# Attention with its division moved behind the product with the values

## The chip, the cores and the metric

The kernel runs on one core of a Trainium2 chip. Five engines work side by side, each through its own list of instructions in order: PE (TensorE, matrix products and transposes into PSUM), DVE (VectorE), ACT (ScalarE), POOL (GpSimd) and SP (SyncE, which issues the transfers). They wait for each other by semaphores. The metric is the device time of one launch in microseconds; lower is better.

## The reference, cut to what matters

```python
def sm_attn(qq, kk, vv):                       # on means of 4 rows: 144 x 144 per head
    s = scale * np.matmul(qq, kk.transpose(0, 1, 3, 2))
    a = np.exp(s - np.max(s, axis=-1, keepdims=True))
    a = a / (np.sum(a, axis=-1, keepdims=True) + 1e-09)
    return np.matmul(a, vv)
out_up = np.repeat(sm_attn(q_d, k_d, v_d), 4, axis=2)
...
scores = np.where(mask, scale * q @ k.T, -1e9)  # 576 x 576 per head, |i - j| < 4
attn = np.exp(scores - max); attn = attn / (sum + 1e-09)
x = out_up + attn @ v                           # (2, 8, 576, 64) -> 1152 rows of 512
...
x = (h * tanh(softplus(h))) @ w_out             # h = x @ w_in, 2048 wide
out = sum over 8 experts of P[:, e] * (relu(x @ w1[e]) @ w2[e])
```

Batch 2, 8 heads, 576 positions, head width 64. The attention is a small part of the arithmetic; the two feed-forward stages behind it are most of it.

## The kernel before

**Stages.** A start (attention of the first 288 tokens), then a feed-forward stage whose products are mixed with the rest of the attention, then the experts. The feed-forward goes through chunks: `gemm1(s)` is 12 products (L506) into a PSUM bank of the tag `w`, `mish` the activation over ACT, POOL and DVE (L486 to L494), and `gemm2(s-4)` 12 products (L529) into banks of the tag `acc`. Large products are done in two parts (hi and lo) for accuracy.

**Units.** Attention is cut into units of three steps: `sc` (scores, row maxima, exponentials), `tr` (transposes to bring the keys onto the partitions) and `av` (product with the values). A `lunit` is 96 queries of the local attention against a window of 102 keys, 8 heads; there are 12. A `gunit` is 72 averaged queries of 4 heads against 144 averaged keys; there are 8. `softmax` (L294 to L308) takes the maxima (L300), runs one exponential for each head with its sum as a by-product (L302, the sums go to the tile `den`, named `ld` or `gd`), adds 1e-9 (L304), takes reciprocals (L305) and multiplies the exponentials by them (L307): two DVE operations a unit, one for each parity `par` of the heads, on 96 x 408 or 72 x 288 numbers. `tr` transposes by PE (L379, L335) and ACT copies the result out (L380, L337). `av` multiplies by the values (L386, L347). For a gunit ACT copies the result to `odT` (L349); for a lunit DVE adds `odT` to it (L392), ACT rounds it to `xhi` (L393) and DVE takes the rest to `xlo` (L394). `xhi` and `xlo` are what L506 reads.

**Waves.** Three waves follow the start. Wave i does three lunits and two gunits, with the transposes of q and k (`prep`, L267), while chunks 6i to 6i+5 of the feed-forward run. At the end of a wave what is left of its steps is issued before the next chunk, since that chunk reads the tokens of the wave (chunks 0, 6, 12 and 18 are the first to read new tokens). The third wave is followed by chunks without attention.

**What sets the order.** Python writes the steps into slots between the products (`pump`), and a scheduler in the framework then orders the instructions on each engine by its own model of time, so that an edit also changes the order around it. Banks of the tag `w` (4 of them) are shared by scores, transposes, `av`, `prep` and `gemm1`; a bank of `gemm1` is held until L490. In the start, short products of a constant (`warm`, L442) fill PE's gaps.

**Weights of the feed-forward** arrive as 64-bit numbers and are converted by ACT (L180) and DVE (L181, L183, L184), then split (L190, L191); the buffers that they arrive in are two, so a transfer waits for the L184 that read the buffer last.

Of the kernel before, what the change touches and what calls it, by code (L numbers as in the profile page):

```python
# [7 lines left out]
F32 = mybir.dt.float32  # L8
# [3 lines left out]
AF = mybir.ActivationFunctionType  # L12
ALU = mybir.AluOpType
# [25 lines left out]
def attn_moe_moe_kernel(  # L39
# [62 lines left out]
    POOL.affine_select(out=maskb, in_=maskb, pattern=[[-1, W + 6]], base=9, channel_multiplier=1,  # L102
                       compare_op=ALU.is_ge, fill=NEG)
    vwt = [at.tile([W, H, D], F32, name=f"vw{i}", bufs=1) for i in range(VWB)]
    pl = [at.tile([TQ, H // 2, W], F32, name=f"pl{i}", bufs=1) for i in range(PBL)]
    pg = [at.tile([SH, H // 4, SD], F32, name=f"pg{i}", bufs=1) for i in range(PBG)]
    DVE.memset(two, 2.0)
    DVE.memset(ones, 1.0)
# [185 lines left out]
    def softmax(s3, p, rows, tag):  # L294

        n, nh, nk = s3[0].shape
        den = new(at, [n, 2, nh], F32, tag + "d", 2)
        for par in range(2):
            nm = new(at, [n, nh], F32, tag + "m", 4)
            DVE.tensor_reduce(out=nm, in_=s3[par], axis=AX.X, op=ALU.max, negate=True)  # L300
            for i in range(nh):
                exps.append(ACT.activation(out=p[par][:, i], in_=s3[par][:, i], func=AF.Exp, bias=nm[:, i:i + 1],  # L302
                                           scale=1.0, accum_out=den[:, par, i:i + 1]))
        DVE.tensor_scalar(out=den, in0=den, scalar1=1e-9, scalar2=rows, op0=ALU.add, op1=ALU.mult)  # L304
        DVE.reciprocal(out=den, in_=den)  # L305
        for par in range(2):
            DVE.tensor_tensor(  # L307
                out=p[par], in0=p[par], in1=den[:, par].unsqueeze(2).to_broadcast([n, nh, nk]), op=ALU.mult)  # L308

    def gunit(b, half, q4):  # L310


        u = {}
        hps = (2 * q4, 2 * q4 + 1)

        def sc():
            bks = [at_bank() for _ in range(2)]
            for i, hp in enumerate(hps):
                for par, bk in enumerate(bks):
                    o = slice(64 * par, 64 * par + 64)  # L320
                    PE.matmul(out=bk[:SH, SD * i:SD * i + SD], lhsT=qd[b, half][o, hp, :], rhs=kd[b][o, hp, :],
                              start=True, stop=True)
            for par in range(2):
                u[par] = pg[state["pg"] % PBG]
                state["pg"] += 1
            softmax([bk[:SH, 0:2 * SD].rearrange("p (a b) -> p a b", b=SD) for bk in bks], u, 4.0, "g")

        def tr():
            u["pt"] = new(at, [W, 8 * TQ], F32, "pt", 2)[:SH, 0:8 * SH].rearrange("p (a b) -> p a b", a=8)
            for par in range(2):  # L330
                bk = at_bank()
                for i in range(2):
                    for c in range(2):
                        j = 2 * i + c
                        PE.transpose(out=bk[:SH, SH * j:SH * j + SH], in_=u[par][:, i, SH * c:SH * c + SH],  # L335
                                     identity=ident[:SH, :SH])
                ACT.activation(out=u["pt"][:, 4 * par:4 * par + 4, :].rearrange("p a b -> p (a b)"),  # L337
                               in_=bk[:SH, 0:4 * SH], func=AF.Copy)

        def av():  # L340
            if (b, half) not in odT:
                odT[b, half] = new(at, [128, HP, SH], F32, "odT", 1)
            bk = at_bank()
            for i, hp in enumerate(hps):
                for c in range(2):
                    for par in range(2):
                        PE.matmul(out=bk[64 * par:64 * par + 64, SH * i:SH * i + SH], lhsT=vd[b, c][:, 2 * hp + par, :],  # L347
                                  rhs=u["pt"][:, 4 * par + 2 * i + c, :], start=(c == 0), stop=(c == 1))
            ACT.activation(out=odT[b, half][:, hps[0]:hps[0] + 2, :].rearrange("p a b -> p (a b)"),  # L349
                           in_=bk[:, 0:2 * SH], func=AF.Copy)  # L350
        return [sc, tr, av]

    def lunit(t):
# [6 lines left out]
        def sc():  # L360
# [7 lines left out]
                    PE.matmul(out=s3[par][:, hp, :], lhsT=qT[b, half][o, hp, TQ * t3:TQ * t3 + TQ],  # L368
                              rhs=kT[b][o, hp, lo:hi], start=False, stop=(hp == HP - 1))
            for par in range(2):  # L370
                u[par] = pl[(2 * t + par) % PBL]
            softmax(s3, u, 1.0, "l")

        def tr():
            u["pt"] = new(at, [W, 8 * TQ], F32, "pt", 2)
            for par in range(2):
                bk = at_bank()
                for i in range(HP):
                    PE.transpose(out=bk[:W, TQ * i:TQ * i + TQ], in_=u[par][:, i, :], identity=ident[:TQ, :TQ])  # L379
                ACT.activation(out=u["pt"][:, 4 * TQ * par:4 * TQ * par + 4 * TQ], in_=bk[:W, 0:4 * TQ], func=AF.Copy)  # L380

        def av():
            bk = at_bank()
# [5 lines left out]
            y4 = bk[:, 0:KD * TQ].rearrange("p (a s r) -> p a s r", a=KD, r=4)  # L389
            g = odT[b, half][:, :, 24 * t3:24 * t3 + 24]  # L390
            hi_, lo_ = (z[:, :, TQ * t:TQ * t + TQ] for z in (xhi, xlo))
            DVE.tensor_tensor(out=y4, in0=y4, in1=g.unsqueeze(3).to_broadcast([128, KD, 24, 4]), op=ALU.add)  # L392
            ACT.activation(out=hi_, in_=y, func=AF.Copy)  # L393
            DVE.tensor_tensor(out=lo_, in0=y, in1=f32(hi_), op=ALU.subtract)  # L394
# [497 lines left out]
```

## Time and profile before

| | us |
|---|---|
| median of 3 runs | 1111.71 (1108.79 to 1116.67) |
| the profiled execution | 1111.02 |
| its span | 1109.2 |
| PE busy | 1077.7 (97%) |
| DVE busy | 579.6 (52%) |
| ACT busy | 487.8 (44%) |
| POOL busy | 368.9 (33%) |

The span is the time from the first to the last instruction in the profile; 1.8 us of the execution lie outside of it. PE is counted as busy also while products in flight drain and while it works at half its clock, so its share doesn't say that it is at its peak. The attention is over at about 186 us of the span, and everything behind it is alike before and after the change.

### The profile page before, as it was taken

How to read it: one execution, taken by the hardware profiler on the slowest of the kernel's cores; microseconds unless marked ns; L12 is line 12 of the kernel's file. 1: busy time of each engine (PE TensorE's matmuls, PEld its weight loads, DVE VectorE, ACT ScalarE, POOL GpSimd, SP SyncE). 2: the span in 40 equal slices, each digit the busy share in tenths (PEclk: the TensorE clock that was granted, in tenths of full speed). 3: DMA queues.
4: the chain of work that ended last, by engine and by line, in shares of the span. 5: the costliest groups of instructions: out<-in, count | busy, mean ns of one | idle time of the engine just before them, and what ended most of it. 6: DMA issues, size and time to landing. Idle time of an engine off the chain costs nothing.

```text
span 1109.2 us, 18583 instructions
## 1 busy us (share of the span) xinstructions
PE 1077.7 (97%) x7184; PEld 983.7 (89%) x7184; DVE 579.6 (52%) x1229; ACT 487.8 (44%) x1375; POOL 368.9 (33%) x406
## 2 busy tenths in 40 slices
PE   8889999999998999999999999999999999999998
PEld 7768789999998888988989898999888999889897
DVE  4877885545347554454454544435454444444442
ACT  3776777534446443424344242442424434243430
POOL 2444523402217335705134150431505224051300
PEclk9888999999999999999999999999999999999999
DMA  8374320222002102112011111201112011120002
GB/s 189 107 154 120 102 81 20 77 80 74 20 1 76 58 1 77 39 38 76 13 66 39 38 40 38 76 19 58 39 38 76 20 58 38 39 71 20 25 1 86
DMA packets 60196, 63.48 MB, mean 57 GB/s; under 512 B 24204, under 2 KB 44620, under 8 KB 60108
## 3 DMA queue, kind: packets, MB, share of 16 engines
q1 hardware_dynamic: 60108, 62.30, 18.8%
q8 instruction: 56, 0.92, 0.3%
q14 instruction: 32, 0.26, 0.1%
HBM read 59.93 MB, written 2.36 MB: 56 GB/s over the span
## 4 chain that ended last, share of the span: by engine, by line
PE 87%; DVE 4%; ACT 3%; POOL 2%; DMA 2%; issue 1%; POOLq 0%; DVEq 0%
PE w L821 36%; PE acc L783 26%; PE w L506 9%; PE acc L529 8%; PE w L783 4%; PE w L368 1%; ACT pl L302 1%; DMA raw<-in_k_dram 1%; PE acc L442 1%; DMA raw<-in_moe_w_out_dram 0%; POOL wc L695 0%; PE w L363 0%; PE w L379 0%; ACT raw L180 0%; POOL me L487 0%
## 5 line engine op out<-in xcount | busy, mean ns | idle before, releaser
L821 PE MATMUL w<-wc,hhi 128*128 128x512 f32 x1152 | 361.9, 393 | 0.0
L821 PEld LDWEIGHTS w<-wc,hhi 128*128 128x128 f32 x1152 | 210.4, 188 | 37.8
L821 PE MATMUL w<-wc,hlo 128*128 128x512 f32 x576 | 225.2, 391 | 0.0
L695 POOL TENSOR_TENSOR wc<-raw,wc 128x512 fp32r<-128x512 f32 x64 | 82.0, 1305 | 356.1 <-ACT wc L694 355.9
L783 PE MATMUL acc<-thi,wb 128*128 128x288 f32 x768 | 169.0, 295 | 0.0
L783 PE MATMUL acc<-xhi,wb 128*128 128x288 f32 x768 | 167.2, 295 | 1.7 <-DVE xlo L557 1.7
L832 DVE SCALAR_TENSOR_TENSOR yacc<-w,P,yacc 128x512 f32<-128x512 f32 x126 | 94.3, 749 | 81.1 <-PE w L821 81.1
L783 PEld LDWEIGHTS acc<-thi,wb 128*128 128x128 f32 x768 | 128.4, 188 | 3.1
L783 PEld LDWEIGHTS acc<-xhi,wb 128*128 128x128 f32 x768 | 128.1, 188 | 3.1 <-DVE xlo L557 1.9
L821 PEld LDWEIGHTS w<-wc,hlo 128*128 128x128 f32 x576 | 108.1, 188 | 23.8
L770 ACT ACTIVATE p<-acc 128x288 f32<-128x288 f32 x128 | 52.3, 410 | 143.2 <-PE acc L783 139.3
L774 ACT ACTIVATE hhi<-acc 128x288 fp32r<-128x288 f32 x128 | 52.3, 410 | 141.5 <-PE acc L783 117.3
L783 PE MATMUL acc<-xlo,wb 128*128 128x288 f32 x384 | 113.5, 295 | 0.0
L783 PE MATMUL acc<-tlo,wb 128*128 128x288 f32 x384 | 113.1, 295 | 0.0
L683 POOL TENSOR_TENSOR wb<-sums,wb 128x256 fp32r<-128x256 f32 x128 | 93.6, 748 | 53.5 <-ACT wb L682 52.1
L683 POOL TENSOR_TENSOR wb<-raw,wb 128x256 fp32r<-128x256 f32 x96 | 72.5, 758 | 97.4 <-PE acc L783 55.5
L775 DVE SCALAR_TENSOR_TENSOR hlo<-acc,hhi 128x288 fp32r<-128x288 f32 x128 | 58.2, 455 | 77.4 <-ACT hhi L774 74.9
L506 PE MATMUL w<-xhi,hi 128*128 128x288 f32 x256 | 79.4, 311 | 5.3 <-ACT xhi L393 2.9
L506 PE MATMUL w<-xlo,hi 128*128 128x288 f32 x256 | 77.7, 304 | 0.1
L529 PE MATMUL acc<-glo,hi 128*128 128x288 f32 x256 | 76.1, 303 | 1.4 <-POOL glo L494 1.4
L506 PE MATMUL w<-xhi,lo 128*128 128x288 f32 x256 | 77.3, 302 | 0.0
L796 DVE TENSOR_TENSOR acc<-acc,u 128x288 f32<-128x288 f32 x64 | 29.6, 464 | 87.7 <-PE acc L783 87.7
(192 smaller groups left out, 1992.9 us busy)
## 6 DMA issues: line engine op xcount, KB each, us to landing
raw<-in_moe_w_dram SPq DMA_DIRECT2D x64, 512.0 KB
raw<-in_moe_w_in_dram SPq DMA_DIRECT2D x16, 512.0 KB
raw<-in_moe_w_out_dram SPq DMA_DIRECT2D x16, 512.0 KB
vw<-in_v_dram SPq DMA_DIRECT2D x12, 192.0 KB
raw<-in_v_dram SPq DMA_DIRECT2D x8, 288.0 KB
raw<-in_q_dram SPq DMA_DIRECT2D x12, 144.0 KB
out_dram<-yacc SPq DMA_DIRECT2D x6, 256.0 KB
raw<-in_k_dram SPq DMA_DIRECT2D x2, 576.0 KB
```

What stands on the lines that cost most here:

```text
L302: exps.append(ACT.activation(out=p[par][:, i], in_=s3[par][:, i], func=AF.Exp, bias=nm[:, i:i + 1], scale=1.0, accum_out=den[:, par, i:i + ...
L506: PE.matmul(out=bk, lhsT=a[:, kk, o], rhs=b[:, kk, c0:c0 + n], start=(i == 0), stop=(i == 3 * KD - 1))
L529: PE.matmul(out=bk, lhsT=a[:, h, o], rhs=b, start=(first and i == 0), stop=(end and i == 2))
L683: POOL.tensor_tensor(out=t[:, 1], in0=src[u][w], in1=f32(t[:, 0]), op=ALU.subtract)
L695: POOL.tensor_tensor(out=t[:, 1], in0=r[:, a], in1=f32(t[:, 0]), op=ALU.subtract)
L770: ACT.activation(out=t, in_=bk[u, b], func=AF.Copy)
L774: ACT.activation(out=hi, in_=y, func=AF.Relu)
L775: DVE.scalar_tensor_tensor(out=lo, in0=y, scalar=0.0, in1=f32(hi), op0=ALU.max, op1=ALU.subtract)
L783: PE.matmul(out=bk[u, b], lhsT=wb[2 * h + u, w][:, wz, kk, :], rhs=ops[xz][:, k + kk, o + c:o + c + NP], start=(m < 3 and i == 0), stop=(i ...
L796: DVE.tensor_tensor(out=bk[u, "C"], in0=bk[u, "C"], in1=kept[u, "u2"], op=ALU.add)
L821: PE.matmul(out=bk, lhsT=a[:, f, 128 * j:128 * j + 128], rhs=w[:, b, :], start=(i == 0), stop=(i == 3 * FH - 1))
L832: DVE.scalar_tensor_tensor(out=y, in0=bk, scalar=p, in1=y, op0=ALU.mult, op1=ALU.add)
```

## The change

The exponentials go undivided into the transposes and the product with the values. The reciprocals of the sums are laid out over partitions by PE: in `spread`, a product with the column of reciprocals, repeated 64 times, as the weights and the identity as the moving operand puts the reciprocal of each query into 64 partitions of a PSUM bank. A lunit does 8 such products (64 x 96) in `tr`, into a bank of its own, which ACT copies into the exponentials' tile (now 128 partitions high); in `av` DVE multiplies the product with the values by it. A gunit does 4 (64 x 72) in `av`, into the free half of the same bank, and DVE multiplies `odT` by them in place, after ACT's copy. The tiles of sums have 4 buffers instead of 2.

```diff
     def softmax(s3, p, rows, tag):
...
-        den = new(at, [n, 2, nh], F32, tag + "d", 2)
+        den = new(at, [n, 2, nh], F32, tag + "d", 4)
...
         DVE.reciprocal(out=den, in_=den)
+        return den
+
+    def spread(bk, c, den, i):
+
+        n = den.shape[0]
         for par in range(2):
-            DVE.tensor_tensor(
-                out=p[par], in0=p[par], in1=den[:, par].unsqueeze(2).to_broadcast([n, nh, nk]), op=ALU.mult)
+            PE.matmul(out=bk[64 * par:64 * par + 64, c:c + n], lhsT=den[:, par, i:i + 1].to_broadcast([n, D]),
+                      rhs=ident[:n, :n], start=True, stop=True)
...
-            ACT.activation(out=odT[b, half][:, hps[0]:hps[0] + 2, :].rearrange("p a b -> p (a b)"),
-                           in_=bk[:, 0:2 * SH], func=AF.Copy)
+                spread(bk, 2 * SH + SH * i, u["den"], i)
+            z = odT[b, half][:, hps[0]:hps[0] + 2, :].rearrange("p a b -> p (a b)")
+            ACT.activation(out=z, in_=bk[:, 0:2 * SH], func=AF.Copy)
+            DVE.tensor_tensor(out=z, in0=bk[:, 2 * SH:4 * SH], in1=z, op=ALU.mult)
...
                 ACT.activation(out=u["pt"][:, 4 * TQ * par:4 * TQ * par + 4 * TQ], in_=bk[:W, 0:4 * TQ], func=AF.Copy)
+            bk = at_bank()
+            for hp in range(HP):
+                spread(bk, TQ * hp, u["den"], hp)
+            u["r"] = pl[2 * t % PBL].rearrange("p a b -> p (a b)")[:, 0:KD * TQ]
+            ACT.activation(out=u["r"], in_=bk[:, 0:KD * TQ], func=AF.Copy)
...
+            DVE.tensor_tensor(out=bk[:, 0:KD * TQ], in0=bk[:, 0:KD * TQ], in1=u["r"], op=ALU.mult)
             DVE.tensor_tensor(out=y4, in0=y4, in1=g.unsqueeze(3).to_broadcast([128, KD, 24, 4]), op=ALU.add)
```

Thirteen lines are added, so a line of the new kernel has a higher number: the spread is L312, the lunit's ACT copy L392, its multiplication L404, the gunit's L357, and old L379, L386, L392, L394, L488, L490, L506 and L529 are L386, L398, L405, L407, L501, L503, L519 and L542.

The scheduler's order changes with it. First, DVE in the first wave, where the first lunit's sums are done; `ld` are the lunit's sums, `lm` its maxima, `raw` a weight under conversion, `mm` a step of mish. Before:

```order
L304 TENSOR_SCALAR ld<-ld 96x8
L305 RECIPROCAL ld<-ld 96x8
L300 TENSOR_REDUCE lm<-w 96x4
L307 TENSOR_TENSOR pl_94<-pl_94,ld 96x408
L307 TENSOR_TENSOR pl_95<-pl_95,ld 96x408
L300 TENSOR_REDUCE lm<-w 96x4
L181 TENSOR_SCALAR raw<-raw 128x512
L488 SCALAR_TENSOR_TENSOR mm<-me 128x288
```

The same place now:

```order
L304 TENSOR_SCALAR ld<-ld 96x8
L305 RECIPROCAL ld<-ld 96x8
L300 TENSOR_REDUCE lm<-w 96x4
L181 TENSOR_SCALAR raw<-raw 128x512
L300 TENSOR_REDUCE lm<-w 96x4
L183 SCALAR_TENSOR_TENSOR raw<-raw_860,raw 128x512
L184 SCALAR_TENSOR_TENSOR raw<-raw_860,raw 128x512
L501 SCALAR_TENSOR_TENSOR mm<-me 128x288
```

The two multiplications are gone, and mish's step has come behind all three steps of the weight's conversion instead of the first.

Second, PE at the end of the second wave; `vw` are the values of a unit's window. Before, the product with the values of the last two lunits is followed by the first product of the next wave's tokens:

```order
L379 MATMUL w<-ident,pl_98 102x96 x4
L379 MATMUL w<-ident,pl_99 102x96 x4
L386 MATMUL w<-pt,vw_92 64x96 x8
L386 MATMUL w<-pt,vw_93 64x96 x8
L506 MATMUL w<-xhi,hi_797 128x288
```

Now 12 products of `gemm2` stand between, of which the first five are:

```order
L386 MATMUL w<-ident,pl_99 102x96 x4
L312 MATMUL w<-ident,ld 64x96 x8
L398 MATMUL w<-pt,vw_92 64x96 x8
L398 MATMUL w<-pt,vw_93 64x96 x8
L542 MATMUL acc<-ghi,hi_1446 128x288 x4
L542 MATMUL acc<-glo,hi_1446 128x288
```

At the end of the third wave it is the other way about: 12 products of `gemm2` stood there before, and 8 do now. Third, DVE at that end, from the second lunit's `av` on. Before:

```order
L392 TENSOR_TENSOR w<-w,odT 128x384 x2
L488 SCALAR_TENSOR_TENSOR mm<-me 128x288
L394 TENSOR_TENSOR xlo<-w,xhi 128x4x96
L490 TENSOR_TENSOR me<-mm,w 128x288
L394 TENSOR_TENSOR xlo<-w,xhi 128x4x96
```

Now:

```order
L404 TENSOR_TENSOR w<-w,pl_96 128x384
L501 SCALAR_TENSOR_TENSOR mm<-me 128x288
L405 TENSOR_TENSOR w<-w,odT 128x384
L404 TENSOR_TENSOR w<-w,pl_98 128x384
L503 TENSOR_TENSOR me<-mm,w 128x288
L405 TENSOR_TENSOR w<-w,odT 128x384
L407 TENSOR_TENSOR xlo<-w,xhi 128x4x96
L505 TENSOR_TENSOR me<-me,ml 128x288
L407 TENSOR_TENSOR xlo<-w,xhi 128x4x96
```

Between the last `av` and the last `xlo` one multiplication and mish's last step have been added.

## Rows read from the trace of the kernel before

**Rows 1.** Windows by stage: us, busy by engine (x count), PEclk, DMA share, GB/s.

```profile
37.00:47.90 10.90, 8.65 (x100) 7.23 (x100) 8.80 (x17) 8.59 (x21) 4.29 (x3) 0.71 0.46 146
47.90:98.50 50.60, 44.85 (x334) 39.30 (x334) 38.92 (x79) 33.98 (x119) 20.02 (x18) 0.79 0.52 119
98.50:146.50 48.00, 41.70 (x388) 36.33 (x386) 41.19 (x86) 35.54 (x128) 24.47 (x26) 1.00 0.46 128
146.50:186.50 40.00, 39.02 (x353) 35.25 (x353) 30.17 (x69) 29.89 (x114) 11.63 (x12) 0.96 0.15 46
186.50:1109.20 922.70, 911.26 (x5595) 836.76 (x5595) 438.24 (x931) 361.13 (x915) 295.34 (x326) 1.00 0.14 46
```

**Rows 2.** Windows by shorter stretches, where the granted clock is low; columns as above.

```profile
59.40:65.50 6.10, 6.10 (x23) 5.45 (x24) 5.06 (x11) 3.92 (x16) 2.08 (x2) 0.50 0.89 163
...
79.20:91.40 12.20, 12.20 (x83) 10.40 (x81) 9.26 (x17) 7.25 (x28) 4.57 (x4) 0.58 0.25 87
...
144.80:150.20 5.40, 3.69 (x22) 3.69 (x23) 4.92 (x11) 3.09 (x8) 0.80 (x1) 0.74 0.35 77
```

**Rows 3.** Groups of instructions by line and shape: count, busy us, mean ns of one.

```profile
L307 DVE TENSOR_TENSOR pl<-pl,ld 96x408 f32<-96x408 f32 x24 | 17.4, 762 | 0.3
...
L380 ACT ACTIVATE pt<-w 102x384 f32<-102x384 f32 x21 | 9.8, 491 | 3.9 <-PE w L379 2.9 <-PE acc L386 1.1
...
L307 DVE TENSOR_TENSOR pg<-pg,gd 72x288 f32<-72x288 f32 x16 | 8.6, 577 | 0.1
...
L392 DVE TENSOR_TENSOR w<-w,odT 128x384 f32<-128x384 f32 x10 | 5.5, 561 | 2.5 <-PE w L386 2.3
```

**Rows 4.** Timeline of PE in the first wave: start, us, what, idle before.

```profile
76.78 0.87 PE L379 MATMUL w<-ident,pl 96*102 96x96 f32 x8 [0.75 <-ACT pl L302]
78.82 0.40 PE L506 MATMUL w<-xhi,hi 128*128 128x288 f32 x1 [1.17 <-DVE me L490]
...
79.21 0.44 PE L506 MATMUL w<-xhi,lo 128*128 128x288 f32 x1
79.45 0.44 PE L506 MATMUL w<-xhi,hi 128*128 128x288 f32 x1
```

**Rows 5.** Timeline of DVE at the same place.

```profile
74.75 1.86 DVE L307 TENSOR_TENSOR pl<-pl,ld 96x408 f32<-96x408 f32 x2
...
78.33 0.44 DVE L490 TENSOR_TENSOR me<-mm,w 128x288 f32<-128x288 f32 x1
```

**Rows 6.** The chain that ended last, in order of time, third wave.

```profile
176.42 0.65 PE w L347 x16
...
178.42 0.81 PE w L386 x16
...
184.25 0.57 DVE w L392
...
186.00 0.48 DVE xlo L394
...
186.53 0.53 PE w L506 x2
```

**Rows 7.** Timeline of PE at the end of the third wave.

```profile
182.30 0.30 PE L506 MATMUL w<-xlo,hi 128*128 128x288 f32 x1
182.44 0.29 PE L506 MATMUL w<-xhi,lo 128*128 128x288 f32 x1
182.66 1.54 PE L386 MATMUL w<-pt,vw 102*64 102x96 f32 x32
```

**Rows 8.** Timeline of PE at the end of the second wave.

```profile
143.24 1.54 PE L386 MATMUL w<-pt,vw 102*64 102x96 f32 x32
146.51 0.40 PE L506 MATMUL w<-xhi,hi 128*128 128x288 f32 x1 [1.73 <-ACT xhi L393]
```

**Rows 9.** Timeline of PE in the second wave, at the first gunit's transposes.

```profile
121.80 0.41 PE L335 MATMUL w<-ident,pg 72*72 72x72 f32 x4 [0.23 <-DVE pg L307]
122.61 0.45 PE L335 MATMUL w<-ident,pg 72*72 72x72 f32 x4 [0.40 <-DVE pg L307]
```

**Rows 10.** The chain that ended last, at the end of the start.

```profile
42.41 4.26 DMA raw<-in_moe_w_out_dram
```

More of the change, by code (lines that the diff above doesn't have):

```diff
@@ L104, in attn_moe_moe_kernel @@
     vwt = [at.tile([W, H, D], F32, name=f"vw{i}", bufs=1) for i in range(VWB)]
-    pl = [at.tile([TQ, H // 2, W], F32, name=f"pl{i}", bufs=1) for i in range(PBL)]
+    pl = [at.tile([128, H // 2, W], F32, name=f"pl{i}", bufs=1) for i in range(PBL)]
     pg = [at.tile([SH, H // 4, SD], F32, name=f"pg{i}", bufs=1) for i in range(PBG)]
@@ L325, in sc @@
                 state["pg"] += 1
-            softmax([bk[:SH, 0:2 * SD].rearrange("p (a b) -> p a b", b=SD) for bk in bks], u, 4.0, "g")
+            u["den"] = softmax([bk[:SH, 0:2 * SD].rearrange("p (a b) -> p a b", b=SD) for bk in bks], u, 4.0, "g")
         def tr():
@@ L370, in sc @@
             for par in range(2):
-                u[par] = pl[(2 * t + par) % PBL]
-            softmax(s3, u, 1.0, "l")
+                u[par] = pl[(2 * t + par) % PBL][:TQ]
+            u["den"] = softmax(s3, u, 1.0, "l")
         def tr():
```

## The prediction

> **What bounds the kernel now.** I read the windows by stage first [rows 1]. Behind 186.5 us the change touches nothing, and PE fills that part: 911.26 of 922.70 us. What can move is the 186 us ahead of it. There the stages differ. In the third wave (146.5 to 186.5) PE is busy 39.02 of 40.00 us and DVE 30.17: PE sets the time. In the first wave (47.9 to 98.5) PE counts as busy for 44.85 of 50.60 us, but at a granted clock of 0.79, and in the second it is busy 41.70 of 48.00 with DVE at 41.19: in these two the waits between the engines set a good part. Then come the timelines at the places where PE waits, to see for whom. The reader is to see that L307, which the change removes, stands directly in front of PE only in three places [rows 4, 5, 9], and that the ends of the waves hang on DVE and ACT behind the product with the values [rows 6, 8]. Two stretches of the first wave run at half clock, 6.10 us at 0.50 and 12.20 us at 0.58 [rows 2]; in the second of them products start 0.24 us apart, against 0.14 at full clock [rows 4, 7], and it begins after PE has stood still twice within three us [rows 4].
>
> **What the change removes, adds and moves.**
>
> DVE loses 24 x 0.762 + 16 x 0.577 us = 17.4 + 8.6 = 26.0 us, and gains 12 multiplications of the shape of L392, 12 x 0.561 = 6.7 us [rows 3], and 8 smaller ones, which have no row: between nothing and a L392, I take half of one, 8 x 0.28 = 2.2 us. Net 17 us less, where DVE is busy for 119 us between 37 and 186.5 [rows 1]. That is worth something only where DVE is in front of PE.
>
> ACT gains 12 copies of the shape of L380, 12 x 0.491 = 5.9 us [rows 3]. Its share of the waves is 67 to 75% [rows 1], and nothing needs the copy until the multiplication in `av`, a whole step later, so I cost it at nothing in the waves. If that cover is gone, a lunit's end comes 0.49 us later.
>
> PE gains the spread. A lunit's is 8 products with 64 columns of weights and 96 moving columns of 4-byte numbers, as the 8 of its `av`: in the trace 16 records, since each such product is recorded twice, and 0.81 us from the first to what follows [rows 6]. A gunit's is 4 products of the kind of L347, half of a row of 0.65 us, 0.33 us [rows 6]. A wave has three lunits and two gunits: 3 x 0.81 + 2 x 0.33 = 3.1 us a wave, and as much in the start; 12.4 us in all. All of them hang on the reciprocals (L305), which come earlier than L307's result did, so PE should not wait for them.
>
> PE is also made to change between products over the whole array and products over half of its columns more often, at up to 12 places and twice at each. The row shows what the change costs: L386 starts 0.22 us behind the last L506, which started 0.14 us behind the one ahead of it [rows 7], so about 0.09 us. This is inside the 0.81 us, which reaches from what precedes L386 to what follows it. The Trainium skill, TensorEngine Tiling, section Key Properties, has a rule that speaks against this change: a change of the tiling mode drains TensorE. It gives no price; its result is a rival below.
>
> *Start.* PE's extra 3.1 us fall into 37 to 47.9, where the granted clock is 0.71 and PE has 2.25 us to spare [rows 1]: 3.1 / 0.71 - 2.25 = 2.1 us at worst. Against it, the last wait of this stage is a transfer of weights that takes 4.26 us [rows 10] and starts when DVE has converted the weights ahead of it, behind divisions of two lunits (4 x 0.762 = 3.0 us at most) that are no longer there; I read it as about 1 us earlier at best, since ACT's exponentials, which stay, are in front of the same conversion. Between -1.0 and +2.1 I take +0.5.
>
> *First wave.* +3.1 us for PE. Two waits should go. At 76.78 PE had waited 0.75 us for what the row calls ACT's exponentials, long done: it was L307, whose two operations run from 74.75 to 76.61 [rows 4, 5]. At 78.82 it had waited 1.17 us for a bank that L490 frees [rows 4], and L490 came late because it is queued on DVE behind the same L307 [rows 5]. In the new order L490 stands behind L184 as well, but PE has 1.1 us of spread ahead of that bank. Together -1.9 us. The clock: the 12.20 us at half speed that follow cost 6.1 us, and the stillness that preceded them is filled. Whether the clock then holds can't be read; I take it that the stretch shrinks to the length of the other one of this wave, 6.10 us, which saves 3.05 [rows 2]. Bounds: nothing, and the whole 6.1. The wave: 3.1 - 1.9 - 3.05 = -1.9.
>
> *Second wave.* +3.1, and the two waits for the gunit's L307, 0.23 + 0.40 us [rows 9], go: -0.6. At its end PE stood still for 1.73 us between the last `av` and the first product of new tokens [rows 8]. DVE now multiplies first, which puts one operation like L392 more behind the last `av` (+0.56; the one for the lunit ahead of it falls beside the `av`), so the wait would be some 2.4 us with the order of DVE a little less tight; but 12 products of gemm2 have come between, 12 x 0.14 = 1.7 us. That leaves 0.7: -1.0. The stretch behind, 144.8 to 150.2, ran at 0.74 [rows 2], that is 5.4 x 0.26 x 2 = 2.8 us at half clock or 1.4 us lost by it, of which some may come back; I take 0.9, bounds nothing and 1.4. The wave: 3.1 - 0.6 - 1.0 - 0.9 = +0.6.
>
> *Third wave.* +3.1, with no wait for L307 to give back. At its end DVE is on the chain already: L392 at 184.25, the last L394 until 186.48, then PE at 186.53 [rows 6]. Behind the last `av` there is now one multiplication more and mish's last step, 0.56 + 0.4 less what is done beside it, I take +0.5; and 8 instead of 12 products of gemm2 cover the time, 4 x 0.14 = 0.6 us. The wave: 3.1 + 0.5 + 0.6 = +4.2. Bounds +2.5 (half of the spread in gaps of 0.98 us that PE has left, rows 1) and +6 (the clock falls over the wait as it did at 146.5).
>
> **The sum**, against the profiled execution's 1111.0 (1109.2 of span and 1.8 around it; the median is 0.7 above it): +0.5 - 1.9 + 0.6 + 4.2 = +3.4, so 1114.4 us.
>
> **The rivals.**
> 1. *Faster: DVE was the bound ahead of 122 us, and the clock holds.* For it: DVE's 41.19 of 48 us, and that both low stretches of the first wave follow waits. Then the half-speed stretches of the first wave go altogether, another 3.05 + 3.05, the start gains its 1.0 instead of losing 0.5 and the second wave its 1.4 instead of 0.9: 1114.4 - 6.1 - 1.5 - 0.5 = 1106.3. Against it: the mish chain of the first chunks, which no L307 is part of, stays.
> 2. *Slower: the fourth shared bank.* The spread takes one more bank of the tag `w` for each lunit, from its first product until ACT's copy, and DVE's multiplication holds the bank of `av` 0.56 us longer. gemm1 holds its own until L490, and PE takes its list in order: a product that finds no bank stops all behind it. The point from which it decides is a wait of the size seen at 78.82, 1.17 us, once per wave: nothing of the first wave's 1.9 comes back, one such wait in each of the other two, and the clock gains nothing (3.05 + 0.9): 1114.4 + 1.9 + 2.3 + 4.0 = 1122.6. For it: this wait is in the trace already. Against: in the third wave, with the same banks, PE has none.
> 3. *Nothing: the spread lies in PE's gaps.* Ends at 1111. Against it: the third wave has gaps of 1 us for 3.1.
> 4. *Drains, the rule above.* If the 0.09 us come on top at 12 places, twice: +2.2, 1116.6. It is what the rule of the Trainium skill (TensorEngine Tiling, Key Properties) would come to here.
>
> **How the numbers follow.** Chances: the forecast 0.40, rival 1 0.20, rival 2 0.20, rival 3 0.12, rival 4 0.08. The range reaches from below rival 1 (the start and the second wave at their bounds as well) to rival 2: 1104 to 1123. One per cent, 11.1 us, is about what a measurement of this kernel can tell from no change. Faster by that, below 1100.6, needs rival 1 and more: 0.06. Slower by it, above 1122.8, is about half of rival 2: 0.10. Within it 0.84.
>
> **What would show it.** In the new profile: the L312 groups of a lunit take about 0.8 us of PE at full clock; the third wave lasts 44 us; PE goes without a wait from the first lunit's transposes, at about 76 us, into gemm1 and the granted clock of that stretch is higher than 0.58; L404 takes 0.56 us and appears on the chain at the ends of the waves; DVE's busy time falls by 17 us, PE's count rises by 256. The prediction is wrong if the third wave hides the spread, if the clock in the first wave falls at other places for longer, or if the spread waits for banks.

## The result, and the profile after

The changed kernel takes 1120.42 us in the median of 20 runs (1114.38 to 1129.43), the kernel before 1113.6 in 20 beside it (1108.79 to 1117.76): a ratio of 1.0064, 95% interval 1.0048 to 1.0079, so 7 us more. The forecast was 3.4 us more. The sign was right and the time lies within the range; the size was half of it. The profiled execution took 1122.22 us, 1.8 above the median of its runs, and the one before 1111.02, 2.6 below the median of these 20, so the two profiles differ by more than the medians do.

The head of the changed kernel's page: the span, the busy times, and the granted clock in 40 slices.

```profile
span 1120.4 us, 19083 instructions
PE 1085.4 (97%) x7440; PEld 991.1 (88%) x7440; DVE 564.8 (50%) x1209; ACT 493.0 (44%) x1387; POOL 365.7 (33%) x406
PEclk9899899999999999999999999999999999999999
```

PE has 256 records more, as counted ahead; DVE's busy time falls by 14.8 us where 17 were forecast. The stages, as the windows of the changed kernel show them (window, length, then busy time and count of PE, PEld, DVE, ACT and POOL, PE's granted clock, DMA share and GB/s). They are cut at the first product that reads new tokens, as the first three stages of [rows 1] are; the last cut of [rows 1], 186.50 us, lies 0.68 us behind that product (185.82 us).

```profile
37.00:49.16 12.16, 5.55 (x92) 4.37 (x90) 10.42 (x21) 8.22 (x20) 4.12 (x3) 0.91 0.41 130
49.16:95.00 45.84, 42.95 (x403) 38.07 (x403) 29.27 (x69) 33.95 (x120) 17.57 (x17) 0.91 0.60 136
95.00:150.53 55.53, 48.47 (x458) 42.89 (x459) 39.23 (x84) 38.98 (x134) 24.67 (x26) 0.93 0.37 101
150.53:192.61 42.08, 39.47 (x403) 35.25 (x402) 24.29 (x59) 29.85 (x113) 9.71 (x11) 0.97 0.12 39
192.61:1120.43 927.82, 916.54 (x5598) 841.37 (x5598) 439.32 (x932) 360.88 (x915) 294.14 (x326) 0.99 0.14 45
```

Against [rows 1], with 185.82 us as its last cut: the start is 1.25 us longer, the first wave 4.8 us shorter, the second 7.5 us longer, the third 2.8 us longer (it lasts 42.1 us where 44 was forecast). Behind the waves 4.4 us are added where nothing was changed: there the clock of this one execution is 0.99, and 1.00 in the one before.

The new instructions in the same stretch (the count, then busy us and the mean ns of one):

```profile
L312 PE MATMUL w<-ident,ld 96*64 96x96 f32 x176 | 10.6, 262 | 0.3 <-DVE me L503 0.2
L312 PE MATMUL w<-ident,gd 72*64 72x72 f32 x48 | 3.5, 226 | 0.0
L404 DVE TENSOR_TENSOR w<-w,pl 128x384 f32<-128x384 f32 x10 | 5.5, 561 | 4.8 <-PE w L398 4.8
L357 DVE TENSOR_TENSOR odT<-w,odT 128x144 f32<-128x144 f32 x6 | 1.7, 277 | 0.2 <-ACT odT L356 0.2
```

L404 takes the 0.56 us and L357 the 0.28 us that the prediction put down for them, and PE hardly ever waits in front of a spread.

The stretch of the first wave that stood at 0.58 in [rows 2], 79.2 to 91.4 us, in the changed kernel:

```profile
79.20:91.40 12.20, 12.20 (x153) 10.78 (x153) 7.17 (x17) 8.87 (x31) 4.41 (x4) 1.00 0.29 86
```

PE has no gap in it and the clock holds. Of the two waits ahead of it in [rows 4], the one for L490 is gone. The other is still there, with the lunit's division taken out, now right behind the last exponential, and 3.4 us at a clock of 0.50 follow it (74.2 to 77.6 us):

```profile
73.36 0.54 PE L386 MATMUL w<-ident,pl 96*102 96x96 f32 x4 [0.76 <-ACT pl L302]
```

What PE waits for between 37 and 193 us now (its own line and the releaser, us in total, times, the longest):

```profile
PE w L519 <- ACT xhi L406: 7.8, 3, 5.1
PE acc L542 <- ACT ghi L506: 2.5, 1, 2.5
PE acc L542 <- POOL glo L507: 2.3, 2, 1.2
```

The longest one is the end of the start. The chain of waits there, in order of time:

```profile
42.12 0.67 ACT raw L180
43.27 0.69 DVE raw L183
43.97 0.47 DVE xlo L407
44.43 0.47 DVE acc L404
45.83 0.47 DVE w L404
46.77 1.28 DVE raw L183
48.05 0.49 DVE w L405
48.62 0.50 ACT xhi L406
49.16 0.61 PE w L519
```

The reader is to see DVE's list: the new L404 and the addition L405 of the last lunit stand between steps of the weights' conversion (L183), and PE, done with its values, stands still for 5.07 us. At the end of the second wave it is the same chain with mish in it; DVE's rows and the row of PE that waited:

```profile
145.48 1.02 DVE L404 TENSOR_TENSOR w<-w,pl 128x384 f32<-128x384 f32 x2
146.41 0.56 DVE L405 TENSOR_TENSOR w<-w,odT 128x384 f32<-128x384 f32 x1
146.88 0.45 DVE L505 TENSOR_TENSOR me<-me,ml 128x288 f32<-128x288 f32 x1
...
147.94 0.79 PE L542 MATMUL acc<-ghi,hi 128*128 128x288 f32 x4 [2.48 <-ACT ghi L506]
```

PE waited 2.48 us for L506, which rounds what L505 leaves, and L505 stands behind two L404. Most of what the clock took in this wave lies further ahead, behind two waits for L507, the step of mish on POOL (the second one, 1.04 us, at 116.92 us):

```profile
109.63 0.40 PE L542 MATMUL acc<-glo,hi 128*128 128x288 f32 x1 [1.23 <-POOL glo L507]
118.60:125.40 6.80, 6.80 (x34) 6.01 (x33) 4.31 (x8) 4.60 (x21) 2.38 (x3) 0.50 0.25 76
```

At the end of the third wave the chain runs over L404 as well:

```profile
190.59 0.56 DVE w L404
191.15 0.35 DVE me L503
191.50 0.48 DVE w L405
192.07 0.50 ACT xhi L406
192.61 0.67 PE w L519 x3
```

### The profile page after: what moved, and what is told of

The parts are those of the page before. It is cut to its first block, busy times and chain, and to the rows that moved or that the text cites. A ratio compares the mean times of both kernels' runs of the same rounds, so it can differ in the third digit from the quotient of the medians.

```text
span 1120.4 us, 19083 instructions
## 1 busy us (share of the span) xinstructions
PE 1085.4 (97%) x7440; PEld 991.1 (88%) x7440; DVE 564.8 (50%) x1209; ACT 493.0 (44%) x1387; POOL 365.7 (33%) x406
## 4 chain that ended last, share of the span: by engine, by line
PE 87%; DVE 4%; ACT 3%; issue 2%; POOL 2%; DMA 2%; SPq 0%; DVEq 0%; ACTq 0%; POOLq 0%
PE w L834 36%; PE acc L796 26%; PE w L519 9%; PE acc L542 8%; PE w L796 4%; PE w L375 1%; DMA raw<-in_q_dram 1%; DMA raw<-in_v_dram 1%; ACT pl L302 1%; POOL me L500 1%; POOL glo L507 1%; PE w L267 0%; DVE raw L183 0%; PE w L723 0%; PE w L312 0%
## 5 line engine op out<-in xcount | busy, mean ns | idle before, releaser
L696 POOL TENSOR_TENSOR wb<-sums,wb 128x256 fp32r<-128x256 f32 x128 | 93.4, 747 | 55.3 <-ACT wb L695 53.8
L696 POOL TENSOR_TENSOR wb<-raw,wb 128x256 fp32r<-128x256 f32 x96 | 72.2, 754 | 100.3 <-PE acc L796 56.9
L519 PE MATMUL w<-xhi,hi 128*128 128x288 f32 x256 | 78.9, 309 | 9.1 <-ACT xhi L406 7.8
L519 PE MATMUL w<-xlo,hi 128*128 128x288 f32 x256 | 78.4, 306 | 0.0
L542 PE MATMUL acc<-glo,hi 128*128 128x288 f32 x256 | 76.1, 301 | 2.4 <-POOL glo L507 2.3
L519 PE MATMUL w<-xhi,lo 128*128 128x288 f32 x256 | 77.3, 302 | 0.0
```

The source lines that it names most:

```text
L519: PE.matmul(out=bk, lhsT=a[:, kk, o], rhs=b[:, kk, c0:c0 + n], start=(i == 0), stop=(i == 3 * KD - 1))
L542: PE.matmul(out=bk, lhsT=a[:, h, o], rhs=b, start=(first and i == 0), stop=(end and i == 2))
L696: POOL.tensor_tensor(out=t[:, 1], in0=src[u][w], in1=f32(t[:, 0]), op=ALU.subtract)
```

## Experiments

All kernels in one table, so that the texts below can be short. The ratio is to the kernel before, from runs on the same chip. The clock is the mean of the granted clock over a kernel's runs (0.981 for the 82 runs of the kernel before in these comparisons). The lengths of start, waves and rest are read from the windows of its one profiled execution (that of e11 is 3.7 us under the median of its runs, that of e12 3.1 us over it), cut at 37 us and at the first product of each set of new tokens (185.82 us for the end of the third wave of the kernel before). "Still" is the time from 37 us to the end of the third wave in which PE isn't busy; "half" is one minus the granted clock times the length, summed over the same stages, an upper bound for what the clock took, since PE would wait for others in part of it anyway.

| kernel | ratio (95%) | clock | start | wave 1 | wave 2 | wave 3 | rest | still | half |
|---|---|---|---|---|---|---|---|---|---|
| before | 1 | 0.981 | 10.9 | 50.6 | 48.0 | 39.3 | 923.4 | 15.2 | 15.4 |
| changed | 1.0064 (1.0048-1.0079) | 0.987 | 12.2 | 45.8 | 55.5 | 42.1 | 927.8 | 19.2 | 10.1 |
| e1 no multiplication | 1.0089 (1.0072-1.0106) | 0.985 | 10.7 | 47.2 | 55.3 | 43.6 | 927.8 | 19.1 | 11.9 |
| e2 no spread | 0.9981 (0.9963-0.9998) | 0.985 | 10.6 | 50.0 | 50.4 | 37.6 | 924.7 | 13.8 | 18.5 |
| e3 neither | 0.9919 (0.9901-0.9937) | 0.988 | 6.6 | 44.8 | 47.1 | 39.0 | 926.3 | 12.7 | 6.8 |
| e4 before + spread | 1.0063 (1.0044-1.0081) | 0.988 | 13.8 | 50.9 | 50.6 | 42.3 | 925.1 | 17.3 | 10.3 |
| e5 bank, no products | 1.0017 (0.9992-1.0042) | 0.985 | 12.9 | 48.4 | 52.4 | 39.1 | 923.2 | 16.1 | 15.3 |
| e6 spread twice | 1.0068 (1.0041-1.0094) | 0.992 | 15.7 | 47.7 | 54.4 | 41.4 | 923.7 | 14.0 | 6.8 |
| e7 half on POOL | 1.0025 (1.0005-1.0046) | 0.984 | 12.0 | 49.5 | 51.9 | 40.5 | 922.7 | 16.0 | 14.3 |
| e8 weights behind | 1.0080 (1.0053-1.0107) | 0.983 | 7.3 | 56.9 | 53.7 | 41.9 | 924.7 | 18.1 | 15.3 |
| e9 filled waits | 1.0034 (1.0013-1.0055) | 0.992 | 12.3 | 48.2 | 52.1 | 40.6 | 924.4 | 12.8 | 5.1 |
| e10 scalars | 0.9985 (0.9965-1.0005) | 0.984 | 13.7 | 46.5 | 48.2 | 39.3 | 925.1 | 13.5 | 12.8 |
| e11 gunits only | 0.9946 (0.9922-0.9971) | 0.988 | 8.6 | 42.6 | 49.0 | 40.3 | 923.2 | 9.2 | 11.7 |
| e12 gunits only, filled | 0.9926 (0.9901-0.9952) | 0.990 | 10.7 | 46.2 | 47.8 | 38.6 | 927.1 | 8.2 | 11.9 |

**First: the change taken apart.** Four kernels: each of its new parts left out, both left out, and the spread added to the kernel before. In e1, e2, e3 and, further down, e5 nothing is divided; constant scales in ACT's copies of the transposed exponentials keep the values small.

```diff
 # e1: of the changed kernel
-            DVE.tensor_tensor(out=z, in0=bk[:, 2 * SH:4 * SH], in1=z, op=ALU.mult)
...
-            DVE.tensor_tensor(out=bk[:, 0:KD * TQ], in0=bk[:, 0:KD * TQ], in1=u["r"], op=ALU.mult)
 # e2: of the changed kernel; the lunit's bank and ACT's copy of it go too; L404 and L357 multiply by other numbers
-                spread(bk, 2 * SH + SH * i, u["den"], i)
...
-                spread(bk, TQ * hp, u["den"], hp)
 # e3: of the kernel before
-            DVE.tensor_tensor(
-                out=p[par], in0=p[par], in1=den[:, par].unsqueeze(2).to_broadcast([n, nh, nk]), op=ALU.mult)
 # e4: of the kernel before
+                spread(bk, 2 * SH + SH * i, u["den"], i)
...
+            bk = at_bank()
+            for hp in range(HP):
+                spread(bk, TQ * hp, u["den"], hp)
+            ACT.activation(out=u["r"], in_=bk[:, 0:KD * TQ], func=AF.Copy)
```

> The new kernel without its last step: the spread products and ACT's copy of them stay, and the multiplication of the values by them (L357 and L404) is left out, so the values stay undivided (constant scales in the copies of the transposed exponentials keep them small). My theory (the 6.8 us are PE's 12.4 us of spread less what L307's removal gives, plus about 3 us for the longer chain at the ends of the three waves): 1117, 3 us faster than the new kernel. Rival, the chain at the wave ends is the whole loss, the spread lying in gaps: 1113 or less. Rival, the spread alone (products and bank): no change, 1120.

> The new kernel without the spread products, their bank and ACT's copy: the multiplications of L357 and L404 stay but multiply by ones (a lunit) and by the values themselves (a gunit), so nothing is divided. My theory: the spread costs PE some 10 of its 12.4 us, so 1110, 10 us faster than the new kernel and 3 faster than the kernel before. Rival, the multiplications at the wave ends are the loss: 1118 or more. Rival, the order of the list and the clock scatter by some us whatever is edited: anywhere between.

> The kernel before without the division L307 and with nothing in its place: the values stay undivided. It is what the removal alone is worth. The prediction's terms for it: two waits of the first wave 1.9, two of the second 0.6, clock 3 to 4, the start about 1: 1107, 6 us faster than before. Rival, L307 never bounds anything but in those waits: 1111, 2.5 faster. Rival 1 of the prediction (DVE is the bound ahead of 122 us and the clock holds without it): 1102 or less.

> The kernel before with L307 kept, plus the spread products, their bank and ACT's copy, whose results nobody uses. It is what the spread alone costs. The prediction's term for it, PE's own time of 3.1 us a wave and in the start, about 10 to 12 in all: 1124, 10 us slower than before. Rival, it lies in PE's gaps: 1114 to 1117. Rival, the fourth shared bank stops the list by a wait of about 1.2 us in each wave on top: 1128 or more.

Medians: 1121.93, 1110.27, 1103.0 and 1119.32 us. So e1 came out as its last rival had it, no faster than the changed kernel, e2 as expected, e3 4 us and e4 5 us below what was expected of them. The removal alone is worth 9.0 us (7.0 to 11.0, from the ratio and 1113 us), more than any term that I had for it. The stages of e3:

```profile
37.00:43.56 6.56, 3.57 (x52) 2.76 (x53) 6.31 (x12) 5.64 (x14) 2.54 (x2) 1.00 0.41 128
43.56:88.34 44.78, 40.27 (x338) 35.25 (x339) 33.76 (x70) 33.62 (x119) 19.89 (x18) 0.92 0.61 150
88.34:135.45 47.11, 42.22 (x384) 37.28 (x382) 34.02 (x74) 35.02 (x126) 24.84 (x25) 0.96 0.47 121
135.45:174.43 38.98, 38.67 (x351) 34.95 (x351) 23.79 (x57) 29.86 (x114) 10.65 (x12) 0.96 0.15 46
```

PE stands still 2.5 us less than before, in sum the 1.9 + 0.6 of the prediction, but in other places: 1.2 us less in the first wave and 1.4 in the second, 0.6 less in the third and 0.7 more in the start. The rest of the gain can be clock: "half" falls by 8.6, from 15.4 to 6.8, where the prediction put 3.95. The start alone ends 4.35 us earlier.

The spread alone (e4) costs 7.0 us (4.9 to 9.0) on the kernel before and 18.9 us on e3 (1103.0 to 1121.93 with e1). The multiplication alone costs 7.3 us on e3 (to e2) and nothing on top of the spread: e1 without it is no faster than the changed kernel. So the two don't add up. In the start each alone makes the stage as long as the other, 10.6 and 10.7 us against 6.6 with neither and 12.2 with both. My expectation of 3 us for the multiplication fell.

The third wave, which has hardly a gap, is the one place where the cost is plain: 37.6 to 39.3 us in the kernels of this table's first six rows without spread, 42.1 to 43.6 in those with one.

**Second: products or bank, and how much.**

```diff
 # e5: of the changed kernel (a lunit; a gunit likewise)
...
-            for hp in range(HP):
-                spread(bk, TQ * hp, u["den"], hp)
+            PE.matmul(out=bk[:, 0:KD * TQ], lhsT=onesb[:1, :], rhs=onesb[:1, 0:TQ].unsqueeze(1).to_broadcast([1, KD, TQ]),
+                      start=True, stop=True)
 # e6: of the changed kernel, in spread
-        for par in range(2):
+        for par in (0, 1, 0, 1):
```

> The new kernel with nearly all of PE's spread time taken out and the rest kept: a lunit's 8 products become one short bfloat16 product of ones into the same bank, a gunit's 4 become one; the bank, ACT's copy of it and the multiplications stay, and nothing is divided. Theory A, after the first four runs: the spread costs PE's own time at full clock, some 12 us of the 19 between the kernel with neither and the one with the spread, and the bank nothing, so 1108 to 1110. Rival B, the fourth shared bank and its release behind ACT's copy hold the list: 1117 or more. Rival C, the length of DVE's chain behind the values: about 1110 too, but then with the stage times of the run with multiplications and no spread.

> The new kernel with every spread product issued twice, the second over the first: 256 more records for PE in the same bank, no more copies, no more operations on DVE. Theory A (PE's own time, nothing of it hidden): another 12 to 14 us, 1133. Rival, the first dose cost what it did because it moved the order and the clock, and a second one lies where PE waits anyway: 1121 to 1127. If the clock holds better the busier PE is, the dose loses some of its 12 us: 1128 to 1130.

e5: 1113.9 us, 3.6 above e2 and 6.5 below the changed kernel; its third wave is back at 39.1 us and its second at 52.4. So the products cost time of their own, and the bank with ACT's copy something of the order of 4 us, which the intervals of e2 and e5 just fail to separate from nothing. e6 went against theory A altogether: 1120.7 us, the same as with one spread. The second dose in PE's groups, busy time of lunits' and gunits' spread between 37 and 197 us:

```profile
L312 PE MATMUL w<-ident,ld 96*64 96x96 f32 x362 | 17.7, 249 | 0.0
L312 PE MATMUL w<-ident,gd 72*64 72x72 f32 x96 | 5.0, 226 | 0.0
```

The work is there, 22.7 us of busy time against 14.1. It goes into PE's stillness, 14.0 us instead of 19.2, and it comes back by the clock: 0.992 over its runs against 0.987. By the profiles, 192.61 to 196.19 us at the end of the waves is all that 192 lunit and 64 gunit records added, and the rest behind the waves is 4.1 us shorter. The third wave isn't longer either: 41.4 us with two spreads, 42.1 with one.

**Third: DVE's load, and the order.**

```diff
 # e7: of the kernel before
-            DVE.tensor_tensor(
+            (DVE, POOL)[par].tensor_tensor(
                 out=p[par], in0=p[par], in1=den[:, par].unsqueeze(2).to_broadcast([n, nh, nk]), op=ALU.mult)
 # e8: of the changed kernel
-            with tc.issue_after(exps[(8, 16, 31, 31)[2 * i + z]].ins):
+            with tc.issue_after((exps[8], exps[16], last["av"], last["av"])[2 * i + z].ins):
                 w_raw()
 # e10: of the kernel before
-            DVE.tensor_tensor(
-                out=p[par], in0=p[par], in1=den[:, par].unsqueeze(2).to_broadcast([n, nh, nk]), op=ALU.mult)
+            for i in range(nh):
+                DVE.tensor_scalar(out=p[par][:, i], in0=p[par][:, i], scalar1=den[:, par, i:i + 1], scalar2=None,
+                                  op0=ALU.mult)
```

> The kernel before with the division kept, but that of the second parity (half of L307) moved from DVE to POOL, where an operation of this size should take 1.0 to 1.3 us by the 128x288 and 128x512 ones seen there. It takes 13 us off DVE and lets both halves run at once; PE gets nothing to do. If the 10 us that the removal alone gives come from DVE's load and the wait in front of the transposes, 1104 to 1108. Rival, POOL's chain of mish (L487, L494), for which PE already waits here and there, gets longer by as much: 1112 to 1118.

> The new kernel with one thing moved: in the start, the conversion of the second block of weights is released by the last copy to xhi of the lunits and no longer by the last exponential, so that on DVE its steps (L181 to L184) stand behind L404 and L405 and not between them. In the new kernel's trace the start ends at 49.16 us, 5 us after PE's last product with the values. Theory D (the conversion that stands in between takes what the removal would give in the start, which ended at 43.6 in the kernel with neither): the start ends 3 to 4 us earlier and the time is 1116 to 1117. Rival, the conversion is then late for the second block and PE waits there: 1120 or more.

> The kernel before with its division kept on DVE in another form: L307, a product of two tensors with the reciprocals broadcast (762 ns for 96x408), becomes one multiplication by a column of scalars for each head, 4 of 96x102 or 2 of 72x144 in place of one. By the row of a scalar operation of 128x512 (L181, about 0.42 us where it stands alone) four should take 0.5 to 0.6 us and two 0.3: 24 x 0.2 + 16 x 0.25 = 8 to 9 us less on DVE, a third of what the removal takes away. If the time goes with DVE's load as the removal's 9.6 us suggests, 1109 to 1110. Rival, the removal's gain is the order and the clock, which go by no such proportion: 1113 or to either side. Rival, four fixed costs make it longer: 1115.

e7: 1117.0 us, 2.8 slower than before (0.6 to 5.1): the rival. Half of the division moved from DVE to POOL gains nothing. What the relief of DVE is worth by itself this run can't tell, since POOL does 22.0 us more for it (13.8 us in 12 L307 of lunits and 8.2 in 8 of gunits).

e8: 1121.42 us. The start ends at 44.26 us, 4.9 earlier, as theory D had it, and the first wave gives back more than that. The windows of the start and the wave, and of a stretch in it:

```profile
37.00:44.26 7.26, 4.92 (x96) 4.36 (x93) 4.86 (x11) 4.19 (x11) 0.00 (x0) 0.97 0.00 1
44.26:101.14 56.88, 51.48 (x403) 45.35 (x403) 38.67 (x78) 37.59 (x125) 22.94 (x20) 0.76 0.58 135
...
74.60:91.70 17.10, 17.10 (x112) 14.77 (x114) 5.96 (x15) 9.32 (x32) 4.25 (x4) 0.50 0.64 144
```

The DMA share of the start is 0.00: nothing was fetched while the conversion waited. The wave then runs 17.1 us at the lower of PE's two levels, 1.2 GHz. The time is what the rival had. A gain in one stage is no gain yet.

e10: 1112.6 us, no change that can be told (1.7 less; between 3.9 less and 0.6 more). Its price was wrong, and that makes it useful. The scalar form in the whole execution:

```profile
L308 DVE TENSOR_SCALAR pl<-pl,ld 96x102 f32<-96x102 f32 x96 | 27.1, 356 | 0.2
L308 DVE TENSOR_SCALAR pg<-pg,gd 72x144 f32<-72x144 f32 x32 | 11.1, 402 | 0.1
```

That is 38.2 us on DVE against 17.4 + 8.6 = 26.0 for L307 [rows 3]: 12 us more, at no cost in time. The Trainium skill (VectorE: DVE Perf Modes, The perf-mode tier table) has float32 from SBUF at twice the rate in this form; at 102 numbers a piece this trace doesn't show it, 0.28 us of busy time each against 0.19, a quarter of L307's 0.76. So the time doesn't go by the sum of DVE's work, and the removal's gain is hardly made of it.

**Fourth: the stillnesses at the ends.**

```diff
 # e9: of the changed kernel, ahead of gemm1's first product
+        for _ in range({0: 64, 6: 12, 12: 16, 18: 24}.get(s, 0)):
+            with tc.issue_after(last["av"].ins):
+                PE.matmul(out=bk[:, 0:128], lhsT=idle, rhs=idle, start=True, stop=True)
```

> The new kernel with 116 short products of no use (bfloat16, the identity by itself, some 0.06 us each at full clock) put between the last product with the values and the first product of new tokens: 64 at the end of the start, 12, 16 and 24 at the ends of the three waves, where PE stands still for 5.1, 1.0, about 2 and 1.7 us in the new kernel's trace. They go into the bank that the first product writes anyway. Theory E (the half-speed stretches that follow such a stillness are its doing, and the clock is what moves the time between these kernels): the granted clock over the run rises from 0.987 to 0.99 or more, and the time falls by 2 to 5 us, to 1115 to 1118. Rival (the clock goes by the whole stretch ahead and not by this stillness, or its loss lies where PE waits anyway): 1120 or, as the junk is in the way by parts of a us, 1122.

1116.42 us, 4.0 less than the changed kernel by the medians; the ratios, 1.0034 and 1.0064, have intervals that still overlap by a little. The end of the start in its trace:

```profile
44.13 3.75 PE L519 MATMUL w<-ident 128*128 128x128 bf16 x64
...
49.28 0.40 PE L523 MATMUL w<-xhi,hi 128*128 128x288 f32 x1 [0.90 <-ACT xhi L406]
```

The first product of new tokens starts as late as it did (49.28 against 49.16). The first two waves behind it:

```profile
49.28:97.51 48.23, 44.82 (x414) 39.46 (x415) 30.19 (x70) 33.70 (x121) 17.81 (x17) 0.89 0.57 129
97.51:149.62 52.11, 46.08 (x482) 40.86 (x480) 38.87 (x84) 38.69 (x136) 25.57 (x26) 1.00 0.41 108
```

"Half" is 5.1 instead of 10.1 us, the three waves together 2.5 us shorter than without, and the clock over all runs rises from 0.987 to 0.992. That is the size that theory E expects, but not its place: the first wave, right behind the 64 products, is 2.4 us longer than without them and its clock is 0.89 against 0.91, while the second and third wave gain 4.9 us. And 3.4 of the 5.8 us between the two profiles lie behind the waves. The two waits for L507 stand in the second wave here too (1.23 and 1.04 us), and its clock stays at 1.00 all the same. So which stillness brings the clock down isn't shown.

**Fifth: the units apart.** e11 treats the gunits as the changed kernel does and divides the lunits by L307. e12 is e11 with products as in e9 (20, 12, 16 and 16).

```diff
 # e11: of the changed kernel
+        if tag == "l":
+            for par in range(2):
+                DVE.tensor_tensor(
+                    out=p[par], in0=p[par], in1=den[:, par].unsqueeze(2).to_broadcast([n, nh, nk]), op=ALU.mult)
         return den
...
-            for hp in range(HP):
-                spread(bk, TQ * hp, u["den"], hp)
...
-            DVE.tensor_tensor(out=bk[:, 0:KD * TQ], in0=bk[:, 0:KD * TQ], in1=u["r"], op=ALU.mult)
```

> The new treatment for the gunits alone (their spread, 4 short products into a bank that is there anyway, and their multiplication), the lunits divided by L307 as before, so with no fourth bank and no multiplication behind the lunits' values. PE gains 8 x 0.33 = 2.6 us, DVE loses 9.2 and gains 2.2. By parts (the two waits for the gunits' L307 0.6, the rest of the gain on DVE by proportion 2): 1112 to 1114. Rival, the loss of the new kernel sits in the gunits: 1117 or more.

> The best kernel so far (the new treatment for the gunits alone, the lunits divided as before) with 64 of the useless short products between the last product with the values and the first product of new tokens: 20, 12, 16 and 16 at the ends of the start and of the three waves. Theory E (a stillness there brings the clock down behind it): 2 to 4 us less than without them, 1102 to 1104, and a granted clock above 0.988. Rival, the low stretches of that kernel begin ahead of the ends (36.4 us in its trace) and nothing is gained: 1106 to 1107, or 1 us more where the junk is in the way.

e11: 1106.15 us, faster than both kernels, by 6.0 us than before (3.2 to 8.7) and by more than the 1112 to 1114 expected. e12: 1106.15 as well; by ratio 0.9926 against 0.9946, which can't be told apart. The 2 to 4 us of theory E don't show in the medians, and the intervals don't exclude them. The stages of e11:

```profile
37.00:45.61 8.61, 7.42 (x77) 6.27 (x73) 7.10 (x14) 6.27 (x16) 2.54 (x2) 0.50 0.37 125
45.61:88.23 42.62, 39.92 (x351) 35.27 (x351) 36.81 (x77) 33.23 (x119) 20.33 (x18) 0.91 0.63 143
88.23:137.19 48.96, 43.62 (x405) 38.36 (x403) 38.66 (x84) 35.65 (x127) 24.46 (x26) 0.97 0.47 125
137.19:177.46 40.27, 40.27 (x367) 35.88 (x367) 27.47 (x65) 30.29 (x114) 10.58 (x12) 0.96 0.15 46
```

PE stands still 9.2 us here, against 15.2 before and 19.2 in the changed kernel. So the change is two changes with opposite signs: that of the gunits gains about 6 us, that of the lunits, on top of it, loses 13 (the ratios 0.9946 and 1.0064). The lunits' treatment was not run without that of the gunits.

## Why the prediction was right, and where it was off

**The sign** was right, in part by luck. In the prediction it stands on the third wave, where PE has hardly a gap, and the runs bear out that the spread costs time there. I had 3.1 us for it; the kernels that differ by the spread (e4 and before, e1 and e3, changed and e2) differ in that wave by 3.0, 4.6 and 4.5, changed and e5, by the products alone, by 3.0. The other terms were too high: I had +4.2 for the wave and the profile shows +2.8. But the loss as measured stands on the second wave, for which I had +0.6. With that +0.6 the measured +1.25, -4.8 and +2.8 of the other stages add up to about nothing.

**The rivals.** The rival that the spread lies in PE's gaps (3) is out by e4 and by the third wave, the one that the clock holds and the kernel is faster (1) by the result; e3 does come out below its 1106, but e10 speaks against DVE's load as the reason. The fourth shared bank (2) is of the order of 4 us by e5, and not as waits of a spread for a bank. Drains (4): from its first product to what follows, a lunit's spread took 0.71 us at 84.91 us of the trace, between transposes and the values' products, which use 64 columns as it does, and 0.81 at 87.73, between products over the whole array. So both changes of mode are in the 0.81 us put down for it, and nothing came on top; the rule of the Trainium skill (TensorEngine Tiling, Key Properties) has no result of its own here.

**The start**, +0.5 forecast, +1.25 in the profile. I had DVE's relief bring the weights earlier, and it does (L180 at 42.12 us where e3 has 42.47 and the kernel before 46.70). I didn't see that on DVE the converted weights then come between the lunits' last operations.

**The first wave**, -1.9 forecast, -4.8 measured. PE stands still 2.9 us less in it, where I had 1.9, but of my two waits only the one at 78.82 is gone. The one at 76.78, which I put down to L307, is still 0.76 us without it. "Half" of this stage goes from 10.5 to 4.0 us, 6.5 less, where I took 3.05 for the clock and 6.1 as its bound. Both were misread: 12.20 us at 0.58 [rows 2] lose 5.1 us and not 6.1, and shrinking to 6.10 us at 0.50 would have saved 2.05.

**The second wave is the term that failed**: +0.6 forecast, +7.5 measured. It was put together from +3.1 for the spread, -1.6 of waits and -0.9 of clock. The spread's part holds: PE's busy time without "half" grows by 2.7 us. The other two have the wrong sign. PE stands still 7.06 us in this wave where it stood 6.30 [rows 1], 0.75 more, and the clock falls to 0.93 from 1.00, up to 4.0 us. There was no clock to give back in this wave, which ran at 1.00; the low part of the stretch at 0.74 [rows 2] lies behind its end. Of the 4.0 us, 3.4 are lost from 118.6 to 125.4 us, behind the waits for L507, for which I had no term. At the end of the wave I had the wait shrink by 1.0 to 0.7 us. The 0.56 us that I had put down for L404 at the end is two L404 ahead of L405 and L505, and the wait is 2.48 us, longer than the 1.73 before [rows 8]. The products of gemm2 that were to fill this time were themselves what waited, since the first of them read the `ghi` that L506 writes: an order shows what stands between, not that it can run.

**The removal** was undervalued, 2.5 us of waits (right in sum) and 3.95 of clock, against 9.0 measured by e3; **the lunits' new steps** were undervalued by more: 9.7 us of products, ACT's copy at nothing and 0.5 us at an end, against 13, from which what the lunits' removal gives back is already taken off. The sum came out near because both errors were large and of opposite sign, which is luck.

**What stays open.** Multiplication and spread cost 7.3 and 18.9 us alone on e3 and 17.4 together, and a second spread nothing. The table tells part of why. Taken together, start and waves less "still" and less "half" are an estimate of PE's work at full clock: 116 to 118 us for before, e2 and e3, 126 for the changed kernel and e1, 130 for e4, 138 for e6. So a spread costs PE 8 to 12 us each time, not far from the 12.4 forecast, and what differs from kernel to kernel is how long PE stands still and at what clock it works. Why it does is open: every edit also changes the order on all engines, and I can't tell which row of the order makes the lunits' treatment stand still 10 us longer than that of e11. The stages are those of one execution of each kernel, so single stretches of low clock may differ in the next.

## What to carry to other kernels

Read a stage by three numbers: what PE has to do, how long it stands still, and its granted clock; an edit that adds to the first can be paid back by the other two, and one that shortens a stage can lose by them (e6 and e8). Moving a division behind the product paid for the gunits and not for the lunits. That it pays where the result is small and is read late, and not where it lengthens the last chain before everybody's next input, is my reading of the chains; no run separates it from the lunits' longer spread and their bank. When a change does the same thing in two places, run the places apart: here the halves had opposite signs.

## What the runs showed of the hardware

PE's clock is a price of its own. Within the 82 runs of the kernel before, 0.01 less of granted clock goes with 5.8 us more, within the 20 of the changed kernel with 9.6 us. Between kernels it doesn't order the times: the changed kernel is slower than the one before at a higher mean clock, 0.987 against 0.981. With 116 useless products in front of its waits the changed kernel's clock was 0.992 and its median 4 us less (e9); with 64 of them the median of a kernel that stood still half as long stayed the same (e12, at 0.990 against 0.988). A scalar multiplication of 96 x 102 float32 numbers takes DVE about 0.28 us, so four of them are dearer than one operation of 96 x 408 with a broadcast operand.
